# A balanced expert assignment rebuilt: bound instead of range, early choice, four columns a count product, one code per token

## The chip, the cores and the metric

The kernel runs on one core of one Trainium2 chip. The metric is the device time of one execution in microseconds, as the median of several runs. A profile of one further execution gives the span of the instructions and the order of time on each engine: PE (TensorE matrix products; PEld is its weight loading), DVE (VectorE), ACT (ScalarE), POOL (GpSimd), SP (SyncE, which issues transfers), and the DMA queues.

## The reference

Two blocks follow one another. The first is a linear attention with a root-mean-square norm, the second a layer of eight experts whose tokens are assigned greedily and evenly: all pairs of token and expert are taken in falling order of their logit, and a pair counts if the token is free and the expert has fewer than 576 tokens.

```python
q, k, v: (8, 8, 576, 64)    g_norm: (64,)
w_gate: (512, 8)   w1: (8, 512, 1024)   w2: (8, 1024, 512)

kv = einsum('bhsd,bhse->bhde', k, v)
out = einsum('bhsd,bhde->bhse', q, kv)
x = out / sqrt(mean(out*out, -1) + 1e-6) * g_norm     # -> x: (4608, 512)

logits = x @ w_gate                                    # (4608, 8)
order = argsort(-logits.flatten())
for idx in order:
    tok, e = idx // 8, idx % 8
    if assigned[tok] >= 0 or counts[e] >= 576: continue
    assigned[tok] = e; counts[e] += 1

for e in range(8):
    mask = assigned == e
    out[mask] = relu(x[mask] @ w1[e]) @ w2[e]
```

## The kernel before

*Attention.* Batches are loaded in pairs by SP and POOL. `kv_product(b)` makes the products of keys and values and, from the gate weights, the columns that give logits. `token_group(i, j0)` handles three columns of 128 tokens: it transposes q, multiplies, and from the squares (`sq`, `ms`) gets the norm's factor `inv` (L175); POOL scales the rows (`x_sb`, L177) and SP stores them in `x_dram`; DVE scales the logits (`part`, L182) and adds them into `lg` (L186). 12 such groups fill `lg`, 128 partitions by 36 columns by 8 experts (4608 tokens).

*Assignment.* The greedy order is found in eight rounds, and each round closes at least one expert. `choose()` takes for each free token its best open expert (`best`, `mx`). `threshold()` looks for the logit at which the first open expert gets full: in each of 6 steps it lays 44 candidates between two ends, compares all tokens with all of them on DVE (`over`, L316), counts per candidate and expert on PE (36 products of 44 columns, `n_ps`, L323), compares the counts with the room left, sums up how many candidates fill an expert (`k_ps`, L332) and takes the two neighbours as new ends. `assign()` gives the tokens above the upper end their expert, and of those between the ends as many as there is room for (`all_ps`, L363). `fetch(t)` picks the expert that is now closed: its number (`index`, L412) is read by SP, which issues the three transfers of its weights (L417, L419); the rank of each of its tokens is found by products with a triangle (`a_ps`, L423) and with one-hot ranges (`s_ps`, L437), and from these come the row numbers `ids` (L455), with which POOL gathers the rows (`xg`, L460) from `x_dram`. In the last round `rest()` gives out what is left.

*Experts.* `turn(t)` transposes the gathered rows (five blocks, `t_ps`, L485). `layers(t)` runs layer 1 (64 products, `h_ps`, L506), and layer 2 (four blocks of 8 products, `y_ps`, L517, and a half block, L525); ACT and DVE copy the results, and POOL puts the rows (`put`, L490). An f32 product is two records on PE.

*Order.* Attention, `control(0)` and `turn(0)` are ordered by the framework's scheduler. From there PE, DVE and ACT keep the order of the program text, and the assignment for expert t+1 is woven into the products of expert t by hand: each `yield` of `control` gives the PE time (us) that has to be issued before its next part, each product yields its own:

```python
            for used in layers(t):
                ...
                if wait is not None:
                    wait -= used
                    if wait <= 0:
                        wait = next(ctl, None)
```

The turn for expert t+1 stands ahead of the half block of expert t. POOL and SP are ordered by the scheduler throughout. The pools of the assignment and of the experts are placed where attention's pool was, on the right side of SBUF; the weights' pool is on the left.

Of the kernel before, what the change touches and what calls it, by code (L numbers as in the profile page):

```python
# [7 lines left out]
FT = mybir.dt.float32  # L8
# [10 lines left out]
NCAND = 44  # L19
NSTEP = 6  # L20
# [5 lines left out]
def kernel(  # L26
# [31 lines left out]
    wpool = ctx.enter_context(tc.tile_pool(name="wpool", bufs=2, side="left"))  # L58
# [62 lines left out]
    lg = const.tile([P, E, GC], FT, name="lg")  # L121
# [81 lines left out]

    asg = ctx.enter_context(tc.tile_pool(name="asg", bufs=1, side="right"))
# [3 lines left out]
    def bc_e(t):  # L212
        return t.rearrange("p (e o) -> p e o", o=1).to_broadcast([P, E, GC])

    def bc_c(t):
        return t.rearrange("p (o c) -> p o c", o=1).to_broadcast([P, E, GC])

    def small(nm, w=1, dt=FT):
        return asg.tile([P, w], dt, name=nm, tag="s_" + nm, bufs=2)
# [4 lines left out]
    ones_b = asg.tile([P, P], BF, name="ones_b")  # L224
    nc.vector.memset(ones_b, 1.0)
    before = asg.tile([P, P], BF, name="before")
    nc.vector.tensor_scalar(before, in0=row_f, scalar1=iota_p, scalar2=None, op0=AL.is_gt)
    code = asg.tile([P, E], FT, name="code")
    nc.vector.tensor_scalar(code, in0=row_f[:, 0:E], scalar1=-1.0, scalar2=float(E), op0=AL.mult, op1=AL.add)
    inner = asg.tile([P, E, GC], BF, name="inner")  # L230
    nc.vector.memset(inner, 1.0)
    nc.vector.memset(inner[:, :, 0:1], 0.0)
    slot_i = asg.tile([P, NB * P], I32, name="slot_i")
    nc.gpsimd.iota(slot_i, pattern=[[1, NB * P]], base=0, channel_multiplier=0)
    slot_f = asg.tile([P, NB * P], FT, name="slot_f")
    nc.gpsimd.tensor_copy(slot_f, slot_i)
    place_i = asg.tile([P, NB], I32, name="place_i")
    nc.gpsimd.iota(place_i, pattern=[[P, NB]], base=0, channel_multiplier=1)
    place_f = asg.tile([P, NB], FT, name="place_f")
    nc.vector.tensor_copy(place_f, place_i)  # L240


    know = asg.tile([P, 2, GC + 3], BF, name="know")
    for n in range(2):
        nc.vector.tensor_copy(know[:, n, GC + 2:GC + 3], iota_p)


    ends = asg.tile([P, 2], FT, name="ends")
    lgf = lg.rearrange("p e c -> p (e c)")
    nc.vector.tensor_reduce(ends[:, 0:1], lgf, axis=AXX, op=AL.max)  # L250
    nc.vector.tensor_reduce(ends[:, 1:2], lgf, axis=AXX, op=AL.min)
    top = asg.tile([P, 1], FT, name="top")
    bottom = asg.tile([P, 1], FT, name="bottom")
    for n, (t, op) in enumerate(((top, AL.max), (bottom, AL.min))):
        wide = asg.tile([P, P], FT, name="wide", tag="wide", bufs=2)
        nc.vector.tensor_copy(wide, ends[:, n:n + 1].to_broadcast([P, P]))
        end_ps = bank([P, P], "end_ps")
        nc.tensor.transpose(end_ps, wide, ident)
        nc.vector.tensor_reduce(t, end_ps, axis=AXX, op=op)
    above = asg.tile([P, 1], FT, name="above")  # L260
    nc.vector.tensor_tensor(above, top, bottom, op=AL.subtract)
# [32 lines left out]
    code_mx = asg.tile([P, GC], FT, name="code_mx")  # L294

    def choose():


# [280 lines left out]
```

## Time and profile before

| what | us |
|---|---|
| median of 3 runs (lowest, highest) | 846.94 (846.91, 849.73) |
| the profiled execution: its own time | 847.75 |
| its span | 846.0 |
| PE busy, PEld, DVE, ACT, POOL | 714.9, 470.7, 332.4, 152.1, 136.5 |
| attention, to the last logits | 0 to 168 |
| first assignment and gathering | 168 to 237 |
| eight experts | 237 to 836 |

A row of the order of time has the start and the length in us, engine, line, operation, the tiles written and read, shapes, how many instructions are merged in it, and in brackets the idle time of the engine ahead of it with what ended it. A group's row has after the bar its busy us, mean ns of one, and the idle time ahead of it. A row of waits has the us in total, how often, and the longest.

### The profile page before, as it was taken

What the parts mean: (1) busy time and instruction counts of PE and PEld (TensorE: products, weight loads), DVE (VectorE), ACT (ScalarE), POOL (GpSimd) and SP (SyncE); (2) the same over time, 40 slices, a digit from 0 to 9 for tenths busy, and PEclk for the clock granted to TensorE, in tenths of its full rate; (3) what the DMA queues carried; (4) which work ended last, traced back from release to release, by engine and by line L of the source; (5) the groups of instructions that cost most, each with busy time, mean ns of one, the idle gap of its engine ahead of it and who ended that gap; (6) DMA issues with size and microseconds to landing.
All of it is one profiled execution on the core that took longest, in us unless ns stands there. A gap on an engine that the chain in (4) does not pass through costs nothing.

```text
span 846.0 us, 12815 instructions
## 1 busy us (share of the span) xinstructions
PE 714.9 (85%) x5410; PEld 470.7 (56%) x5410; DVE 332.4 (39%) x1033; ACT 152.1 (18%) x310; POOL 136.5 (16%) x119
## 2 busy tenths in 40 slices
PE   0689889513099999999999999999999997999995
PEld 0678778413077447645754674576467545745741
DVE  0064854855725505633570555156235605000000
ACT  0043442400021021102112110211021121202200
POOL 2133523310100210030003003100300031111001
PEclk9899999855599999999999999999999998999998
DMA  9999892100610430070016005300800264200000
GB/s 221 300 243 291 246 295 91 76 38 1 223 32 2 166 139 8 1 284 27 2 57 248 7 2 199 112 2 1 291 20 2 82 223 156 105 25 32 1 25 31
DMA packets 36793, 91.01 MB, mean 108 GB/s; under 512 B 2944, under 2 KB 2944, under 8 KB 36736
## 3 DMA queue, kind: packets, MB, share of 16 engines
q1 hardware_dynamic: 29056, 66.59, 24.0%
q0 software_dynamic: 6976, 23.60, 8.6%
q8 instruction: 42, 0.69, 0.3%
q10 hardware_dynamic: 704, 0.02, 0.1%
q14 instruction: 15, 0.12, 0.0%
HBM read 71.32 MB, written 18.87 MB: 107 GB/s over the span
## 4 chain that ended last, share of the span: by engine, by line
PE 59%; issue 16%; DVE 13%; DMA 6%; ACT 3%; POOL 2%; ACTq 0%; SPq 0%; POOLq 0%; DVEq 0%
PE h_ps L506 24%; PE y_ps L517 17%; PE n_ps L323 6%; DMA v_sb<-in_v_dram 4%; PE o_ps L162 3%; PE y_ps L525 3%; PE kv_ps L131 2%; DVE part L182 2%; DMA w_sb<-in_moe_w_dram 1%; DVE over L316 1%; DVE ms L167 1%; ACT xt L486 1%; PE qt_ps L155 1%; POOL out_dram L490 1%; PE t_ps L485 1%
## 5 line engine op out<-in xcount | busy, mean ns | idle before, releaser
L506 PE MATMUL h_ps<-xt,w_sb 128*128 128x288 f32 x1024 | 273.0, 417 | 0.0
L517 PE MATMUL y_ps<-w_sb,hid 128*128 128x512 f32 x512 | 224.6, 595 | 0.0
L506 PEld LDWEIGHTS h_ps<-xt,w_sb 128*128 128x128 f32 x1024 | 189.4, 191 | 58.2 <-issue 10.6
L517 PEld LDWEIGHTS y_ps<-w_sb,hid 128*128 128x128 f32 x512 | 95.8, 190 | 124.0 <-issue 123.2
L490 POOL DMA_INDIRECT out_dram<-y_sb,ids x40 | 38.7, 966 | 500.0 <-DVE rel L441 293.8
L530 DVE TENSOR_TENSOR y_sb<-y_ps,y_part 64x512 f32<-64x512 f32 x8 | 5.5, 683 | 266.1 <-ACT y_part L529 266.1
L509 ACT ACTIVATE hid<-h_ps 128x288 f32<-128x288 f32 x128 | 52.5, 410 | 260.1 <-PE h_ps L506 258.5
L316 DVE TENSOR_TENSOR over<-mx,cand 128x1584 bf16<-128x1584 f32 x42 | 75.9, 1808 | 1.3
L323 PE MATMUL n_ps<-best,over 128*44 128x8 bf16 x1512 | 50.2, 178 | 19.5 <-DVE over L316 19.5
L323 PEld LDWEIGHTS <-over 128*44 128x44 bf16 x1512 | 46.1, 104 | 36.6 <-DVE over L316 22.7
L131 PE MATMUL kv_ps<-v_sb,k_sb 64*64 64x64 f32 x1152 | 43.0, 235 | 27.5 <-DMA v_sb<-in_v_dram 27.5
L520 ACT COPY y_sb<-y_ps 128x512 f32<-128x512 f32 x32 | 18.7, 585 | 216.3 <-PE y_ps L517 216.3
L131 PEld LDWEIGHTS kv_ps<-v_sb,k_sb 64*64 64x64 f32 x1152 | 40.3, 150 | 30.5 <-issue 25.8
L162 PE MATMUL o_ps<-bd,qt 128*64 128x144 f32 x576 | 46.8, 305 | 11.3 <-DVE qt L157 9.7
L460 POOL DMA_INDIRECT xg<-x_dram,ids x40 | 38.1, 953 | 85.8 <-DVE ids L455 52.0
L162 PEld LDWEIGHTS o_ps<-bd,qt 128*64 128x64 f32 x576 | 38.7, 144 | 15.4 <-ACT o_sb L166 10.5
L177 POOL TENSOR_TENSOR x_sb<-o_sb,inv 128x1536 f32<-128x1536 f32 x12 | 33.2, 2766 | 48.7 <-DVE inv L175 40.1
L326 DVE SCALAR_TENSOR_TENSOR full<-n_ps,goal 44x8 f32<-44x8 f32 x42 | 6.6, 158 | 83.7 <-PE n_ps L323 83.7
L486 ACT ACTIVATE xt<-t_ps,g_col 128x512 f32<-128x512 f32 (+1 forms) x40 | 24.0, 644 | 70.1 <-issue 68.4
L485 PE MATMUL t_ps<-ident,xg 128*128 128x128 f32 (+1 forms) x160 | 23.2, 283 | 14.2 <-DMA xg<-x_dram,ids 9.8
L485 PEld LDWEIGHTS t_ps<-ident,xg 128*128 128x128 f32 (+1 forms) x160 | 18.0, 147 | 23.1 <-DMA xg<-x_dram,ids 9.9
L525 PE MATMUL y_ps<-w_sb,hid 128*64 128x512 f32 x128 | 29.2, 598 | 0.0
(147 smaller groups left out, 466.9 us busy)
## 6 DMA issues: line engine op xcount, KB each, us to landing
w_sb<-in_moe_w_dram SPq DMA_DIRECT2D x16, 1024.0 KB, 6.3
w_sb<-in_moe_w_dram SPq DMA_DIRECT2D x8, 2048.0 KB, 17.3
k_sb<-in_k_dram SPq DMA_DIRECT2D x8, 1152.0 KB, 8.2
v_sb<-in_v_dram SPq DMA_DIRECT2D x8, 1152.0 KB, 12.7
x_dram<-x_sb SPq DMA_DIRECT2D x12, 768.0 KB, 3.8
q_sb<-in_q_dram POOLq DMA_DIRECT2D x4, 1152.0 KB
q_sb<-in_q_dram SPq DMA_DIRECT2D x4, 1152.0 KB
xg<-x_dram,ids POOLq DMA_INDIRECT x40
```

What stands on the lines that cost most here:

```text
L131: nc.tensor.matmul(kv_ps[ls, r, :], lhsT=k_sb[ls, r, j, :], rhs=v_sb[ls, r, j, :], start=(j == 0), stop=(j == R - 1))
L162: nc.tensor.matmul(o_ps[ps_, r, 0:W], lhsT=qt[:, r, ps_], rhs=bd[:, 2 * i + n, r], start=True, stop=True)
L177: nc.gpsimd.tensor_tensor(x_sb.rearrange("p (a l d) -> p a l d", l=2, d=D), o_sb.rearrange("p t r w -> p (t r) w")[:, :, 0:P].rearrange("p ...
L316: nc.vector.tensor_tensor(over, mx.rearrange("p (c o) -> p c o", o=1).to_broadcast([P, GC, NCAND]), cand[:, 1:NCAND + 1].rearrange("p (o n ...
L323: nc.tensor.matmul(n_ps, lhsT=over[:, c, :], rhs=best[:, :, c], start=(c == 0), stop=(c == GC - 1))
L460: nc.gpsimd.indirect_dma_start(out=xg[0:nr, :], out_offset=None, in_=x_dram, in_offset=bass.IndirectOffsetOnAxis(ap=ids[0:nr, n:n + 1], ax ...
L485: nc.tensor.transpose(t_ps[:, d, 0:nr], xg[0:nr, d * P:(d + 1) * P], ident[0:nr, 0:nr])
L490: put = nc.gpsimd.indirect_dma_start(out=out, out_offset=bass.IndirectOffsetOnAxis(ap=ids_of[t][0:nr, n:n + 1], axis=0), in_=y_sb[0:nr, :] ...
L506: nc.tensor.matmul(h_ps, lhsT=w1[:, d, f * P:(f + 1) * P], rhs=xt[:, d, cs], start=(d == 0), stop=(d == DC - 1))
L509: nc.scalar.activation(hid[:, f, cs], h_ps, ACT.Relu)
L517: nc.tensor.matmul(y_ps, lhsT=hid[:, f, a:a + nr], rhs=w2[:, f, :], start=(f == 0), stop=(f == FC - 1))
L525: nc.tensor.matmul(y_ps[l * nr:(l + 1) * nr], lhsT=hid[:, l * FC // 2 + f, a:a + nr], rhs=w2[:, l * FC // 2 + f, :], start=(f == 0), stop= ...
```

## The change

- The logits are no longer searched for their range: from the gate weights comes a bound on any logit (`bound`, with `g2_ps` and a square root), to which the logits are also cut. `top` and `bottom` come from it.
- The pool `asg` moves to the left side and is opened ahead of attention, so that the constants and the first candidates (`cand0`) are made at the start; the weights' pool moves to the right.
- `choose` and the first comparison (`compare` into `over0`) run for columns 0 to 16, 16 to 24, 24 to 32 and 32 to 36 after the token groups that end at columns 18, 24, 33 and 36 (`early`).
- 32 candidates and 7 steps instead of 44 and 6. A count product takes four columns at once: 128 columns of weights (4 columns of tokens by 32 candidates) by 32 streamed (4 by 8 experts); only the four blocks on the diagonal of the result are used, and DVE takes three of them from the room before it compares the fourth.
- `assign` keeps one number per token, `who` (the expert's code), instead of the mask `given`; `index` comes ahead of the tokens' marks; `fetch` compares `who` with the code.
- In `fetch` a difference of ranks (`fall`) replaces the second comparison with 640 slots.
- All yields are set anew; `control(0)` and `turn(0)` are inside the hand-ordered part; expert 0 runs layer 1 by halves of its tokens.

```diff
-NCAND = 44
-NSTEP = 6
+NCAND = 32
+NSTEP = 7
...
-    wpool = ctx.enter_context(tc.tile_pool(name="wpool", bufs=2, side="left"))
+    asg = ctx.enter_context(tc.tile_pool(name="asg", bufs=1, side="left"))
...
+    g2_ps = psa.tile([P, E], FT, name="g2_ps", tag="aux")
+    nc.tensor.matmul(g2_ps, lhsT=ones_f, rhs=g2, start=True, stop=True)
+    bound = asg.tile([P, 1], FT, name="bound")
+    nc.vector.tensor_reduce(bound, g2_ps, axis=AXX, op=AL.max)
+    nc.scalar.activation(bound, bound, ACT.Sqrt)
...
+    def choose(c0=None, c1=GC):
+        cs = slice(c0 or 0, c1)
+        n = cs.stop - cs.start
+        if c0 is None:
+            nc.vector.tensor_tensor(wl, lg, bc_e(shut), op=AL.add)
+        else:
+            nc.vector.tensor_scalar(lg[:, :, cs], in0=lg[:, :, cs], scalar1=bound, scalar2=bottom,
+                                    op0=AL.min, op1=AL.max)
+        w = wl if c0 is None else lg
+        nc.vector.tensor_reduce(mx[:, cs], w[:, :, cs].rearrange("p e c -> p c e"), axis=AXX, op=AL.max)
+        nc.vector.tensor_tensor(pick[:, :, cs], w[:, :, cs], bc_c(mx[:, cs]), op=AL.is_ge)
+        nc.vector.tensor_tensor(pick[:, :, cs], pick[:, :, cs], bc_e(code, n), op=AL.mult)
+        nc.vector.tensor_reduce(code_mx[:, cs], pick[:, :, cs].rearrange("p e c -> p c e"), axis=AXX, op=AL.max)
+        nc.vector.tensor_tensor(best[:, cs].rearrange("p c e -> p e c"), pick[:, :, cs], bc_c(code_mx[:, cs]),
+                                op=AL.is_equal)
+        if c0 is None:
+            nc.vector.tensor_tensor(mx, mx, gone, op=AL.add)
...
         for j0 in range(0, R, T):
             token_group(i, j0)
+            c0 = {18: 0, 24: 16, 33: 24, GC: GC - G}.get(i * R + j0 + T)
+            if c0 is not None:
+                early(c0, (i * R + j0 + T) // G * G)
...
-            yield 6.5 if s == 0 else 2.9
-            n_ps = bank([NCAND, E], "n_ps")
-            for c in range(GC):
-                nc.tensor.matmul(n_ps, lhsT=over[:, c, :], rhs=best[:, :, c], start=(c == 0), stop=(c == GC - 1))
...
-            yield 0.9
+            yield 7.2 if s == 0 else 2.8
+            n_ps = bank([P, G * E], "n_ps")
+            for c in range(0, GC, G):
+                nc.tensor.matmul(n_ps, lhsT=over[:, c:c + G].rearrange("p c n -> p (c n)"),
+                                 rhs=best[:, c:c + G].rearrange("p c e -> p (c e)"),
+                                 start=(c == 0), stop=(c == GC - G))
+            need = goal[0:QP]
+            for g in range(1, G):
+                less = small("need", E)[0:QP]
+                nc.vector.tensor_tensor(less, need, n_ps[g * QP:(g + 1) * QP, g * E:(g + 1) * E], op=AL.subtract)
+                need = less
...
+            yield 1.4
...
-        yield 4.5
+        yield 3.6
+        all_ps = bank([P, 3, E], "all_ps")
...
+        mid = asg.tile([P, E, GC], BF, name="mid", tag="mid")
+        nc.vector.tensor_tensor(mid, two[:, 1], two[:, 0], op=AL.subtract)
...
+        index = small("index", dt=I32)
+        nc.vector.tensor_scalar(index, in0=which, scalar1=-1.0, scalar2=float(E), op0=AL.mult, op1=AL.add)
         nc.vector.tensor_tensor(here, here, bc_e(last), op=AL.is_le)
+        took = small("took", GC)
+        nc.vector.tensor_reduce(took, here.rearrange("p e c -> p c e"), axis=AXX, op=AL.max)
+        nc.vector.tensor_tensor(took, took, cut[:, 0], op=AL.max)
+        mine = small("mine", GC)
+        nc.vector.tensor_tensor(mine, took, code_mx, op=AL.mult)
+        nc.vector.tensor_tensor(who, who, mine, op=AL.max)
...
-        yield 3.0
+        own = small("own", GC)
+        nc.vector.tensor_scalar(own, in0=who, scalar1=which, scalar2=None, op0=AL.is_equal)
+        along = small("along", GC, BF)
+        nc.vector.tensor_tensor_scan(along, ones_b[:, 0:GC], own, 0.0, op0=AL.mult, op1=AL.add)
+        yield 5.5 if t < E - 1 else 8.0
+        a_ps = bank([P, GC + 1], "a_ps")
+        nc.tensor.matmul(a_ps[:, 0:1], lhsT=before, rhs=along[:, GC - 1:GC], start=True, stop=True)
+        nc.tensor.matmul(a_ps[:, 1:GC + 1], lhsT=fall, rhs=along, start=True, stop=True)
...
-        yield 2.4
+        yield 1.5
...
-        for f in range(FC):
-            for c in range(2):
+        for f, c in [(f, c) for f in range(FC) for c in range(2)] if t else [(f, c) for c in range(2) for f in range(FC)]:
+            if True:
...
-    for _ in control(0):
-        pass
-    for _ in turn(0):
-        pass
     with tc.manual_schedule(engines={mybir.EngineType.PE, mybir.EngineType.DVE, mybir.EngineType.Activation}):
+        for _ in control(0):
+            pass
+        for _ in turn(0):
+            pass
```

More of the change, by code (lines that the diff above doesn't have):

```diff
@@ L235 @@
[L235 to L259, printed above, removed]
@@ new lines, in threshold @@
+            nc.tensor.matmul(k_ps, lhsT=ones_b[0:QP, :], rhs=some, start=True, stop=True)
+            ends = small("ends", 2)
+            hi, lo = ends[:, 0:1], ends[:, 1:2]
+            for n in range(2):
+                at = small("at", NCAND + 1)
+                nc.vector.scalar_tensor_tensor(at, in0=row_f[:, 0:NCAND + 1], scalar=k_ps, in1=cand[:, n:NCAND + 1 + n],
+                                               op0=AL.is_equal, op1=AL.mult, accum_out=ends[:, 1 - n:2 - n])
+        return ends
@@ L375, in assign @@
-        nc.vector.tensor_scalar(is_full, in0=room, scalar1=0.5, scalar2=None, op0=AL.is_lt)
+        nc.vector.scalar_tensor_tensor(last, in0=left, scalar=-1.0e6, in1=all_ps[:, 2], op0=AL.add, op1=AL.subtract)
+        fresh = small("fresh", E)
+        nc.vector.scalar_tensor_tensor(fresh, in0=over_room, scalar=0.5, in1=code_left, op0=AL.is_lt, op1=AL.mult)
+        which = small("which")
+        nc.vector.tensor_reduce(which, fresh, axis=AXX, op=AL.max)
+        index = small("index", dt=I32)
```

297 lines of the change are left out of this document (146 added, 151 removed).

## The prediction

> **What bounds the kernel now.** I read the page's slices first, then the busy time by stages, then the order of time of each engine, then the waits. The columns of a stage are its length, then PE, PEld, DVE, ACT and POOL busy (instructions), granted clock, DMA share, GB/s.
>
> ```profile
> DVE  0064854855725505633570555156235605000000
> 174.40:184.20 9.80, 0.66 (x2) 0.29 (x2) 9.30 (x42) 0.00 (x0) 1.24 (x3) 0.50 0.00 0
> 184.20:210.80 26.60, 10.57 (x222) 9.76 (x223) 14.73 (x57) 0.00 (x0) 0.00 (x0) 0.50 0.00 1
> 210.80:237.30 26.50, 4.75 (x29) 3.70 (x28) 15.80 (x56) 2.55 (x4) 4.86 (x5) 0.52 0.56 203
> 314.40:700.00 385.60, 374.15 (x2292) 227.36 (x2290) 168.92 (x570) 61.84 (x130) 47.94 (x50) 1.00 0.24 86
> ```
>
> Attention ends near 168 us. From there to 237 us PE waits for the first assignment, at a granted clock of 0.50: 69 us bound by a chain of small DVE and PE work. From 314.4 to 700 us five experts take 385.60 us, 77.12 us each, and PE is busy for 97% of it: there the time is what stands in PE's queue. So the change counts in two ways: the length of the exposed chain, and the PE time and PE stalls that each later assignment puts among the experts' products.
>
> ```profile
> 161.39 2.76 POOL L177 TENSOR_TENSOR x_sb<-o_sb,inv 128x1536 f32<-128x1536 f32 x1 [3.79 <-DVE inv L175]
> 162.09 2.27 DVE L182 TENSOR_TENSOR part<-o_sb,inv 128x192 f32<-128x192 f32 x1
> 167.28 0.36 DVE L182 TENSOR_TENSOR part<-o_sb,inv 128x192 f32<-128x192 f32 x1
> 167.67 0.50 DVE L186 TENSOR_REDUCE lg<-part 128x24 f32<-128x192 f32 x1
> 167.85 2.76 POOL L177 TENSOR_TENSOR x_sb<-o_sb,inv 128x1536 f32<-128x1536 f32 x1 [3.71 <-DVE part L182]
> 174.43 0.17 DVE L225 MEMSET ones_b<- 128x128 bf16 x1 [6.26 <-DMA x_dram<-x_sb]
> 184.22 1.60 PE L323 MATMUL n_ps<-best,over 128*44 128x8 bf16 x36 [6.61 <-DVE over L316]
> 188.99 1.60 PE L323 MATMUL n_ps<-best,over 128*44 128x8 bf16 x36 [2.57 <-DVE over L316]
> 210.82 0.24 DVE L347 TENSOR_SCALAR cut<-mx,hi 128x36 f32<-128x36 f32 x1
> 217.38 0.15 DVE L412 TENSOR_SCALAR index<-which 128x1 int32<-128x1 f32 x1
> 227.16 0.17 DVE L455 SCALAR_TENSOR_TENSOR ids<-got,col 128x5 int32<-128x5 f32 x1
> 232.96 3.67 PE L485 MATMUL t_ps<-ident,xg 128*128 128x128 f32 x16 [9.77 <-DMA xg<-x_dram,ids]
> 237.26 7.06 PE L506 MATMUL h_ps<-xt,w_sb 128*128 128x288 f32 x28
> ```
>
> The last logits are written at 168.17, but the first instruction of the assignment (`ones_b`) starts at 174.43: it waits for the last store of x to DRAM, because its pool takes the place of attention's. The first count starts at 184.22, a step takes 4.77 us (184.22 to 188.99), the thresholds are done at 210.8, the expert's index at 217.51, the row numbers at 227.33, the first product of layer 1 at 237.3.
>
> ```profile
> 246.57 3.18 PE L506 MATMUL h_ps<-xt,w_sb 128*128 128x288 f32 x12
> 249.68 1.13 PE L323 MATMUL n_ps<-best,over 128*44 128x8 bf16 x36
> 250.74 1.24 PE L506 MATMUL h_ps<-xt,w_sb 128*128 128x288 f32 x4
> 252.01 0.75 PE L506 MATMUL h_ps<-xt,w_sb 128*128 128x288 f32 x2
> 284.05 0.16 PE L423 MATMUL a_ps<-know,before 128*128 128x1 bf16 x1 [1.70 <-DVE index L412]
> 286.73 0.29 PE L437 MATMUL s_ps<-know,of 128*128 128x39 bf16 x5
> 286.87 20.85 PE L517 MATMUL y_ps<-w_sb,hid 128*128 128x512 f32 x48
> 708.32 0.16 PE L423 MATMUL a_ps<-know,before 128*128 128x1 bf16 x1 [4.64 <-DVE index L412]
> 708.34 5.15 PE L506 MATMUL h_ps<-xt,w_sb 128*128 128x288 f32 x10
> 766.52 1.04 PE L485 MATMUL t_ps<-ident,xg 128*128 128x128 f32 x8
> 773.35 31.31 PE L506 MATMUL h_ps<-xt,w_sb 128*128 128x288 f32 x128
> 832.06 3.65 PE L525 MATMUL y_ps<-w_sb,hid 128*64 128x512 f32 x16
> PE a_ps L423 <- DVE index L412: 10.2, 6, 1.7
> ```
>
> This is PE among the experts. One step of a threshold goes from 246.57 to 252.01, 5.44 us, with 16 records (8 products) of layer 1 in it. Expert 7 has no assignment beside it: 128 records take 31.2 us, 0.2435 each, so 8 products are 3.90 us and a step costs 1.54 us of PE: 1.06 for the 36 count products (249.68 to 250.74), 0.48 for `k_ps` and the gaps at the changes between f32 and bf16. Besides, `a_ps` waits 1.7 us for DVE six times (10.2 us), and 4.64 us at 708.32 for the last assignment.
>
> **The change, part by part.**
>
> *Start of the chain.* The pool moves away from attention's, constants are built while attention's first loads run (DVE's first two slices, 42 us, are empty), and the bound comes from the gate weights instead of the logits; the end transposes and most of the 42 DVE instructions of that stage, the choice over all 36 columns among them (174.43 to 182.3), go. What stays behind the last logits is the choice and comparison of four columns: six operations of 32 elements and one of 128. The price of small ones:
>
> ```profile
> L368 DVE TENSOR_TENSOR last<-left,all_ps 128x8 f32<-128x8 f32 x7 | 1.1, 162 | 0.2
> L182 DVE TENSOR_TENSOR part<-o_sb,inv 128x192 f32<-128x192 f32 x12 | 19.6, 1634 | 0.1
> L316 DVE TENSOR_TENSOR over<-mx,cand 128x1584 bf16<-128x1584 f32 x42 | 75.9, 1808 | 1.3
> L406 DVE TENSOR_TENSOR own_e<-given,hot 128x288 bf16<-128x288 bf16 x8 | 3.7, 457 | 0.2
> ```
>
> A dependent small one takes 0.16 and starts 0.04 to 0.1 later, so 0.24 each. But the four two-input ones meet POOL's `x_sb`: `part` takes 0.36 at 167.28, before POOL starts, and 2.27 at 162.09, where it ends with POOL's operation (164.15); the group's mean is 1634 ns. So I take the clip and the first maximum at once, a block until POOL's end at 170.61, then five at 0.27 and 0.04 to PE: 172.0. To this comes what the earlier three parts (16, 8 and 8 columns) cost attention itself: about 2.2, 1.5 and 1.5 us of DVE plus a POOL operation (2.76) in front of each at worst, with the last part 15 us as an upper bound; below, nothing (DVE is given work only). DMA is still the limit for the first part, and DVE has gaps, so nearer to the lower end: 2.5. First count at 174.5 instead of 184.22: -9.7.
>
> *Steps.* Seven instead of six. The comparison falls from 1584 elements (1.81) to 1152; 1.65 x 1152/1584 and 0.16 fixed, 1.36. Nine count products replace 36. At 232 us and before, the clock is half:
>
> ```profile
> 222.84 0.35 PE L437 MATMUL s_ps<-know,of 128*128 128x39 bf16 x5 [2.69 <-DVE know L433]
> 227.61 1.08 POOL L460 DMA_INDIRECT xg<-x_dram,ids  x1 [51.97 <-DVE ids L455]
> 232.78 0.91 POOL L460 DMA_INDIRECT xg<-x_dram,ids  x1 [0.30 <-issue]
> ```
>
> Five `s_ps` products with 128 columns of weights and 39 streamed take 0.35; one alone (`a_ps`) takes 0.16, so they come some 47 ns apart and nine are 0.53, against 1.60. Three subtractions come between count and comparison, 0.20 each. A step: 0.56 count, 0.60, 0.20, 0.20, 0.20 to `k_ps`' readers, 0.38 for both ends, 0.28 for candidates, 1.42 for the comparison: 3.84. Six of them and a last one without candidates and comparison (2.3) are 25.3 against 26.6 (184.22 to 210.8): -1.3, and -2.5 to +1 if a subtraction is 0.15 or 0.3.
>
> *Split.* From the ends to the index: 0.28 for both cuts, 0.87 for two products, 0.79 and 0.1 for the sums, then, ahead of the room in DVE's order, the difference, the scan and the scaled sum (1.63), and 1.05 for six small ones: 4.7 against 6.7: -2.0. From the index to the row numbers no other work is mixed in any more, and one comparison of 36 codes replaces product and reduction over 288: 6.2 against 9.8. The rows come no sooner than DMA allows: the weights' 4 MB start with the index and the gathers meet them. Before, the last gather was issued at 232.78 and layer 1 began at 237.3. Bounds: 0 (rows held until the weights are in) and -3.6 (all of it); gathers have a queue of their own, so I take -3.0. In expert 0 the order of layer 1 by halves changes nothing, since all turning products stand ahead of it.
>
> *Among the experts.* Per step PE does nine products. Warm, five `s_ps` go from 286.73 to 286.87, 28 ns each: 0.26 for nine against 1.06. With `k_ps` and the gaps a step is 0.74, seven 5.2, against 9.3. The rest: `all_ps`, `a_ps`, `s_ps` 0.5 with no stall. Base without assignment: 773.35 to 835.65 is 62.3, and the turn and its gaps 766.52 to 769.77, 3.25: 65.5. So 71.2 instead of 77.12: -5.9, six times -35.5. Between a count and the one before, `k_ps` to count is paced by six products (2.92) for 0.47 + 0.28 + 1.36 = 2.1 of DVE; count to `k_ps` by three (1.46) for 1.0; `a_ps` by seven of layer 2 (6.0, at 0.434 a record) for 3.4; the first count by 15 (7.3) for some 6.6: 1.35 until `y_sb` is added, seven operations of the choice with 288 elements at 0.45 to 0.65, then candidates and comparison. These covers hold the edits that cost nothing; without them each costs its whole DVE time.
>
> *Last assignment.* 8.0 of pacing is 17 products (8.28) for 6.5 of DVE: the stall of 4.64 goes, and what followed it: ten records took 5.15 instead of 2.44 at a clock that had fallen. 65.5 + 0.5 against 73.3 (700.0 to 773.35): -7.3.
>
> *What moves.* The index comes after ten products of layer 2 instead of one, and the row numbers after 19 instead of 8: 13 products, 11.2 us, remain to the turn. SP then issues three weight transfers, POOL five gathers of 1.25 us each behind two of the output puts.
>
> ```profile
> w_sb<-in_moe_w_dram SPq DMA_DIRECT2D x8, 2048.0 KB, 17.3
> ```
>
> The weights land 17.3 after issue and layer 1 of the next expert starts some 19 after the index's issue, but needs `w2` 31 us later still: covered. The last gather is issued 2.9 + 5.0 us after `s_ps` and may take 4.5 (232.78 to 237.3 holds its landing, turning and copy): 12.4, needed at 11.2 + 2.85 = 14.0. Covered by 1.6 us only.
>
> Sum: 9.7 + 1.3 + 2.0 + 3.0 + 35.5 + 7.3 = 58.8. The profiled execution took 847.75 (span 846.0): 789.0, and the median 846.94 is 0.8 below it: 788.
>
> **A rule against it.** A count product loads 128 columns of weights where it loaded 44. By the rows the load hides: 28 ns for 128 columns (`s_ps`) and 29 for 44. The Trainium skill, TensorE: Matmul & The Clock Gate, LDWEIGHTS, has the load's time grow with its columns, P/1.2 ns, 107 ns for 128. By that nine are 0.96 and the sum would be about 30 us smaller. The trace's `s_ps` row does not bear it out.
>
> **The rivals.**
> - *Weights by column.* If a count product were paid by its weight columns, 1.06/36 x 128/44 = 86 ns, nine are 0.77, +0.51 on 42 warm steps and +0.55 on seven cold ones: +25.6, 814. For it: 44-column loads at half clock need 41 ns each. Against: both `s_ps` rows. 6%.
> - *Gathers late.* If the gathers, 8 us later in layer 2, share DMA worse than I take, PE waits at the turn: 2 us at each of six, 12 in all: 800. For it: DMA was busy for 0.56 of 26.5 us in expert 0's start, 14.8 us, and the gathers now come in the middle of such a stretch. 13%.
> - *Attention pays.* All four parts at their upper bound, 15 instead of 2.5: 801. For it: the 1634 ns of `part`. Against: DVE's gaps there. 8%.
> - *Slower.* POOL's queue is in order and not written by hand. If the put of layer 2's fourth block stands ahead of the gathers, they start after 32 products: 0.65 + 1.3 + 5.0 to the last issue and 4.5 to its use, where 2.85 was due, so PE waits some 9 us at each of six turns, with clocks lost as at 708 (2.7 each): +70, 858. It decides from 9.8 us lost per turn. Against: gathers are ready at the 22nd product, that put at the 33rd. 3%.
> - *No effect.* The stalls only move, from `a_ps` to the next wait: 10.2 + 4.64 and the 2.7 of clock stay, 17.5: 806. For it: the split's chain is barely shorter. Against: seven products of cover instead of four. 4%.
>
> **How the numbers follow.** My forecast 64%, with 781 to 796 by its own bounds: attention 0 to 8, gathers -3.6 to 0, gaps 0.28 to 0.39 a step. The range takes in late gathers and attention's price: 780 to 806. No measurement of this kernel tells less than 0.5% (4 us) from no change. Faster: all but the slower rival and 2% for what I do not see, 0.95; same 0.02, slower 0.03.
>
> **What would show it.** The first count near 174.5 and 3.8 us a step; layer 1 of expert 0 near 221; 71.2 us from expert to expert; `n_ps` groups of nine in some 0.4 with their tail; no wait of `a_ps` for DVE; no wait of `t_ps` for gathers beyond the first. Wrong it is if `n_ps` groups take 0.9, if PE's waits name `over`, `some` or the gathers, or if attention ends after 172.

## The result, and the profile after

The runs of each kernel are compared with runs of the kernel before on the same chip.

| kernel | median us (lowest, highest) | ratio to before, 95% interval |
|---|---|---|
| before, beside after | 848.34 (846.91, 850.56) | |
| after | 790.33 (789.52, 792.82) | 0.9319 (0.9286 to 0.9352) |

The forecast was 788.0, within 780 to 806. After's profiled execution took 792.82 (span 791.0) against before's 847.75 (846.0): 54.9 us less between the two profiles. The page's slices and the same stages as before, of after (columns: length, PE, PEld, DVE, ACT, POOL busy, granted clock, DMA share, GB/s):

```profile
DVE  0364746587825625562663455165445514000000
177.70:182.40 4.70, 0.20 (x2) 0.20 (x2) 4.07 (x13) 0.00 (x0) 2.06 (x1) 0.50 0.41 166
182.40:205.10 22.70, 3.63 (x61) 2.49 (x60) 17.27 (x82) 0.00 (x0) 0.00 (x0) 0.50 0.01 1
205.10:229.60 24.50, 5.58 (x31) 3.89 (x31) 15.55 (x51) 2.59 (x4) 6.23 (x5) 0.50 0.60 219
301.30:652.60 351.30, 348.42 (x1542) 206.87 (x1540) 171.91 (x690) 61.82 (x130) 48.78 (x50) 1.00 0.27 94
```

DVE's second slice (about 20 to 40 us), empty before, has work in it now; the first is still empty. Five experts take 351.30 us where they took 385.60, 70.26 each, with 750 PE records fewer; PE is busy for 99% of it. The order of time of after's exposed chain (PE and DVE):

```profile
177.18 0.50 DVE L319 TENSOR_REDUCE lg<-part 128x24 f32<-128x192 f32 x1
177.72 2.08 DVE L225 TENSOR_SCALAR lg<-lg,bound,bottom 128x32 f32<-128x32 f32 x1
181.20 0.18 PE L364 MATMUL n_ps<-best,over 128*128 128x32 bf16 x1 [4.42 <-DVE best L232]
184.64 0.42 PE L364 MATMUL n_ps<-best,over 128*128 128x32 bf16 x9 [2.09 <-DVE cand L358]
188.32 0.42 PE L364 MATMUL n_ps<-best,over 128*128 128x32 bf16 x9 [2.09 <-DVE cand L358]
205.15 0.23 DVE L392 TENSOR_TENSOR cut<-mx,ends 128x72 bf16<-128x72 f32 x1
209.78 0.15 DVE L425 TENSOR_SCALAR index<-which 128x1 int32<-128x1 f32 x1
229.58 9.04 PE L552 MATMUL h_ps<-xt,w_sb 128*128 128x288 f32 x30
```

Against the rows of before that the prediction shows, the thresholds are done at 205.15 instead of 210.82, the index comes at 209.78 instead of 217.38, layer 1 of expert 0 starts at 229.58 instead of 237.26. But the last logits are written at 177.68 instead of 168.17. Attention itself became 9.5 us longer, and where the rows come from is seen here (after, DVE, POOL and PE):

```profile
102.22 0.50 DVE L319 TENSOR_REDUCE lg<-part 128x24 f32<-128x192 f32 x1
102.03 2.78 POOL L310 TENSOR_TENSOR x_sb<-o_sb,inv 128x1536 f32<-128x1536 f32 x1 [2.98 <-DVE inv L308]
102.76 2.13 DVE L225 TENSOR_SCALAR lg<-lg,bound,bottom 128x128 f32<-128x128 f32 x1
106.34 0.41 DVE L266 COPY bd<-kv_ps 64x256 f32<-64x256 f32 x1
107.20 1.12 PE L270 MATMUL t_ps<-ident,bd 128*128 128x128 f32 x4 [5.05 <-ACT bd L267]
111.33 6.20 PE L264 MATMUL kv_ps<-v_sb,k_sb 64*64 64x64 f32 x124
```

The same place in before:

```profile
102.64 0.40 DVE L133 COPY bd<-kv_ps 64x256 f32<-64x256 f32 x1
103.50 0.66 PE L137 MATMUL t_ps<-ident,bd 128*128 128x128 f32 x4 [1.34 <-ACT bd L134]
105.83 3.83 PE L131 MATMUL kv_ps<-v_sb,k_sb 64*64 64x64 f32 x124
```

Up to 102.7 the two kernels run alike. Then the first early part stands in DVE's queue ahead of the copy `bd`. Its first operation, the clip of the logits to the bound, takes 2.13 us: it ends with POOL's `x_sb` (104.81). `bd` comes 3.70 us later, PE waits 5.05 instead of 1.34 us, and after that wait the same 124 records of `kv_ps` take 6.20 instead of 3.83 us, at a granted clock of 0.50 from 107.2 to 116 us where before has 1.00 (over the stretch from 100 to 120 us the mean is 0.74 against 1.00). So 3.6 us of DVE time ahead of `bd` cost 7.9 us: `kv_ps` ends at 117.53 instead of 109.66.

Among the experts (after, PE):

```profile
281.27 0.17 PE L475 MATMUL a_ps<-along,before 128*128 128x1 bf16 x1
294.49 1.04 PE L530 MATMUL t_ps<-ident,xg 128*128 128x128 f32 x8
313.69 0.38 PE L364 MATMUL n_ps<-best,over 128*128 128x32 bf16 x9
313.92 1.70 PE L552 MATMUL h_ps<-xt,w_sb 128*128 128x288 f32 x6
315.65 3.18 PE L552 MATMUL h_ps<-xt,w_sb 128*128 128x288 f32 x12
318.67 0.38 PE L364 MATMUL n_ps<-best,over 128*128 128x32 bf16 x9
652.60 8.51 PE L552 MATMUL h_ps<-xt,w_sb 128*128 128x288 f32 x34
660.95 0.17 PE L475 MATMUL a_ps<-along,before 128*128 128x1 bf16 x1
718.40 6.82 PE L552 MATMUL h_ps<-xt,w_sb 128*128 128x288 f32 x27
```

A step is 4.98 us (313.69 to 318.67) with 18 records of layer 1 in it; at 0.2435 a record these are 4.38, so the step costs PE 0.60. Nine count products hold it for 0.23 (313.69 to 313.92), 26 ns each. Neither `a_ps` row has idle time, and the turn at 294.49 has none ahead of it: both the old stall and the late gathers are absent. In the waits of PE over the whole execution, `a_ps` (4.3 us) and `t_ps` (0.6 us for the gathers) each wait once, both ahead of expert 0.

### The profile page after: what moved, and what is told of

It is laid out like the page before. It is cut to its first block, busy times and chain, and to the rows that moved or that the text cites. A ratio compares the mean times of both kernels' runs of the same rounds, so it can differ in the third digit from the quotient of the medians.

```text
span 791.0 us, 10903 instructions
## 1 busy us (share of the span) xinstructions
PE 681.3 (86%) x4361; PEld 443.4 (56%) x4361; DVE 344.7 (44%) x1214; ACT 151.1 (19%) x310; POOL 138.3 (17%) x118
## 4 chain that ended last, share of the span: by engine, by line
PE 59%; issue 19%; DVE 11%; DMA 5%; ACT 2%; POOL 2%; POOLq 0%; ACTq 0%; DVEq 0%
PE h_ps L552 27%; PE y_ps L563 16%; PE o_ps L295 4%; DMA v_sb<-in_v_dram 4%; PE kv_ps L264 3%; PE y_ps L571 3%; DVE part L315 2%; PE n_ps L364 1%; DVE ms L300 1%; PE qt_ps L288 1%; DVE over L238 1%; PE w_ps L275 1%; POOL out_dram L535 1%; PE t_ps L530 1%; ACT xt L531 1%
## 5 line engine op out<-in xcount | busy, mean ns | idle before, releaser
L563 PE MATMUL y_ps<-w_sb,hid 128*128 128x512 f32 x512 | 227.2, 597 | 0.0
L535 POOL DMA_INDIRECT out_dram<-y_sb,ids x40 | 39.7, 993 | 441.3 <-ACT y_sb L566 390.7
L238 DVE TENSOR_TENSOR over<-mx,cand 128x1152 bf16<-128x1152 f32 (+3 forms) x52 | 67.0, 1289 | 1.6
L264 PE MATMUL kv_ps<-v_sb,k_sb 64*64 64x64 f32 x1152 | 45.2, 242 | 0.1
L264 PEld LDWEIGHTS kv_ps<-v_sb,k_sb 64*64 64x64 f32 x1152 | 42.4, 156 | 3.2 <-issue 2.9
L364 PEld LDWEIGHTS <-over 128*128 128x128 bf16 x441 | 18.1, 97 | 38.4 <-DVE over L238 22.4
L370 DVE TENSOR_TENSOR need<-goal,n_ps 32x8 f32<-32x8 f32 x49 | 7.5, 154 | 69.0 <-PE n_ps L364 69.0
L364 PE MATMUL n_ps<-best,over 128*128 128x32 bf16 x441 | 19.2, 178 | 21.4 <-DVE cand L358 12.5
L385 DVE SCALAR_TENSOR_TENSOR at<-row_f,k_ps,cand 128x33 f32<-128x33 f32 x98 | 21.5, 257 | 34.3 <-PE k_ps L380 34.3
```

Of the source, the lines that this page charges most:

```text
L238: nc.vector.tensor_tensor(over[:, c0:c1], mx[:, c0:c1].rearrange("p (c o) -> p c o", o=1).to_broadcast([P, c1 - c0, NCAND]), cand[:, 1:NCA ...
L264: nc.tensor.matmul(kv_ps[ls, r, :], lhsT=k_sb[ls, r, j, :], rhs=v_sb[ls, r, j, :], start=(j == 0), stop=(j == R - 1))
L364: nc.tensor.matmul(n_ps, lhsT=over[:, c:c + G].rearrange("p c n -> p (c n)"), rhs=best[:, c:c + G].rearrange("p c e -> p (c e)"), start=(c ...
L535: put = nc.gpsimd.indirect_dma_start(out=out, out_offset=bass.IndirectOffsetOnAxis(ap=ids_of[t][0:nr, n:n + 1], axis=0), in_=y_sb[0:nr, :] ...
L563: nc.tensor.matmul(y_ps, lhsT=hid[:, f, a:a + nr], rhs=w2[:, f, :], start=(f == 0), stop=(f == FC - 1))
```

## The experiments

**The first early part.** `e1_gap` makes it wait for batch 4's logit columns, `e2_noearly` has no early part at all.

```diff
+        if i == 2:
+            late = asg.tile([P, 1], FT, name="late")
+            nc.vector.scalar_tensor_tensor(late, in0=bd[:, 4, 0, P:P + 1], scalar=0.0, in1=bound, ...)
+            early(0, 16, late)
-            c0 = {18: 0, 24: 16, 33: 24, GC: GC - G}.get(i * R + j0 + T)
+            c0 = {24: 16, 33: 24, GC: GC - G}.get(i * R + j0 + T)      # e1_gap
+            c0 = {GC: 0}.get(i * R + j0 + T)                           # e2_noearly; it has no `if i == 2` part
...
```

> The first early part (columns 0 to 16) is made to wait for the logit columns of batch 4, so that DVE does it in its gap beside PE's next products of keys and values, when POOL is idle. Theory A (the clip to the bound is held by POOL's x_sb for 2.1 us, the copy that PE waits for comes 3.7 us late behind it, PE idles 5 us and then runs at half clock, 4.2 us more): PE's products of the fifth batch take 3.8 us again instead of 6.1, the last logits come near 170 us instead of 177.7, and the time falls by 7.5 from 790.3 to 783. Theory B (DVE's added work costs attention the same wherever it stands): 789 to 790, last logits still near 177.

> No early parts: choice and first comparison for all 36 columns after the last logits, everything else as in the changed kernel. Theory A: last logits near 168.5, then the clip waits for POOL until 171, choice and comparison take 5.5, first k_ps near 177 instead of 182.4: 785, so the early parts are a loss of 5 us. Theory C (attention is later because of the constants and the bound at its start, not because of the early parts): last logits near 177, first k_ps near 186: 794.

`e1_gap`: 783.09 us (782.83 to 784.74), ratio 0.9256 (0.9231 to 0.9281). `e2_noearly`: 784.86 (782.51 to 786.11), 0.9264 (0.9234 to 0.9293). In the order of time of `e1_gap`:

```profile
105.79 0.35 DVE L225 TENSOR_SCALAR lg<-lg,late,bottom 128x128 f32<-128x128 f32 x1
105.23 3.83 PE L264 MATMUL kv_ps<-v_sb,k_sb 64*64 64x64 f32 x124
168.56 0.50 DVE L319 TENSOR_REDUCE lg<-part 128x24 f32<-128x192 f32 x1
```

The clip of the same 128 columns takes 0.35 without POOL beside it, `kv_ps` runs in 3.83 again, and the last logits come at 169.06, 0.9 us after before's. In `e2_noearly` they come at 167.11, but the choice over 36 columns then stands in the chain:

```profile
174.35 0.42 PE L364 MATMUL n_ps<-best,over 128*128 128x32 bf16 x9 [12.87 <-DVE best L232]
```

So the early parts, as placed, lose more than they bring: without them the kernel is 5.5 us faster by the medians (the intervals, 0.9234 to 0.9293 and 0.9286 to 0.9352, just touch), and layer 1 of expert 0 starts at 222.82 instead of 229.58. That moving the first part alone brings the gain is clear of the scatter (`e1_gap` ends at 0.9281). What the parts are worth when well placed is not: 1.8 us by the medians (784.86 to 783.09, inside the runs' scatter), 2.1 by the start of layer 1 (222.82 and 220.68).

**What halves the speed of `kv_ps`.** `e7_warm` puts products that nothing reads (20 of them) into PE's queue behind the sixth token group.

```diff
+            if i * R + j0 + T == 18:
...
+                for _ in range(20):
+                    nc.tensor.matmul(warm, lhsT=ident, rhs=inv, start=True, stop=True)
```

> Twenty products whose result nobody reads stand in PE's queue where it waits for the first early part (they need the norm's factor, ready at 101.8). DVE's order is unchanged, so the copy that PE waits for still comes near 106.4. Theory A (of the 7.9 us, 4.2 are PE's clock, which falls in the idle time): PE's products of the fifth batch take 3.8 us instead of 6.1, last logits near 174, time 786. Theory E (the products are slow because DVE or DMA feed them late): they still take 6 us, 790.

790.5 us, one execution. The order of time on PE and DVE:

```profile
98.82 7.61 PE L337 MATMUL warm<-inv,ident 128*128 128x24 f32 x40 [2.00 <-DVE inv L308]
106.36 2.61 PE L264 MATMUL kv_ps<-v_sb,k_sb 64*64 64x64 f32 x42
109.01 0.42 DVE L266 COPY bd<-kv_ps 64x256 f32<-64x256 f32 x1 [5.21 <-PE kv_ps L264]
112.77 3.83 PE L264 MATMUL kv_ps<-v_sb,k_sb 64*64 64x64 f32 x124
```

The edit does more than keep PE at work. The filling products stand ahead of the last 42 `kv_ps` records that `bd` needs, so `bd` comes 9.27 us after the clip's start, where it was 3.58 in after, and the time is no evidence. The granted clock fell here too: it is 0.50 from 100 to 110 us, while PE is busy with the filling products, behind 2.00 us of idle time. It is back at 1.00 when the 124 records start, and they take 3.83 although `bd` was later than in after. So the clock, and not a late feed by DVE or DMA (whose share is near 1.0 beside the 124 records in both), makes them slow in after.

That the idle time lets the clock fall is not shown by this run, only by comparing the others. In the seven profiles with the first part ahead of `bd` and no filling (after, `e3_last`, `e4_hold`, `e6_single`, `e8_flat`, `e10_act`, `e13_w2`), PE waits 3.51 to 5.06 us for `bd`, and the 124 records take 5.10 to 6.54. In the six with `bd` first (before, `e5_pace`, `e1_gap`, `e2_noearly`, `e11_best`, `e12_both`) it waits 1.34 or 1.35, and they take 3.83. In between the length alone does not decide: in before, the granted clock is 0.53 behind 2.14 us of idle time at 126.88, and 1.00 behind 2.06 at 94.56.

**POOL's hold on the last part.** `e3_last` issues the last `x_sb` behind the last early part; `e10_act` lets ACT scale those rows.

```diff
+            if i * R + j0 + T == GC:
+                rows()        # e3_last: x_sb and its store for the last group, held back by best
...
+        if i * R + j0 + T == GC:      # e10_act
+            for k in range(T * H):
+                nc.scalar.mul(x_sb[:, k * D:(k + 1) * D], o_sb[:, t, r, l * D:(l + 1) * D], inv[:, k:k + 1])
```

> POOL scales the last three columns of rows only after the last early part is done (its factor is copied behind that part). Theory A: the last clip takes 0.2 instead of 2.08, first k_ps at 180.5 instead of 182.4, the rows are in DRAM 4 us later, 30 us before the first gather: 1.8 us less, 788.5. Theory D (the end of the chain to layer 1 is set by transfers, not by the assignment): layer 1 starts at 229.6 as now, 790.

> After, with one operation moved: the rows x of the last token group are scaled by ACT (24 pieces of 64 columns) instead of POOL, so that no POOL operation runs while DVE does the last clip, choice and comparison. Theory A (POOL's operation holds DVE's clip, 2.08 us against 0.30 without POOL): the last clip takes 0.3, the first two threshold steps come 3.68 apart as the others, and from the end of the last logits to all_ps it takes 28.2 us instead of 30.0; the time falls by 1.8, to about 788.5. Rival B (the 2.08 us are the clip's own, or come from the store of the rows): the clip stays at 2.1 and the stretch at 30.0. Rival C (ACT's pieces make the rows late for the gathers): layer 1 of expert 0 comes later after the index than 19.8 us.

`e3_last`: 790.31 us in one execution. The clip took 0.30 there, but POOL then held a later operation of the first step, `at`, which finds one of the two new ends (1.81 us, the next one 0.25), and the count behind that came late:

```profile
177.57 2.76 POOL L324 TENSOR_TENSOR x_sb<-o_sb,inv_late 128x1536 f32<-128x1536 f32 x1 [6.66 <-DVE need L382]
178.56 1.81 DVE L397 SCALAR_TENSOR_TENSOR at<-row_f,k_ps,cand 128x33 f32<-128x33 f32 x1 [0.25 <-PE k_ps L392]
182.17 0.42 PE L376 MATMUL n_ps<-best,over 128*128 128x32 bf16 x9 [3.65 <-DVE cand L370]
```

3.65 instead of 2.09 us: the block moved, and from the last logits to `all_ps` it took 29.76 instead of after's 30.01. `e10_act` (788.32, one execution) takes POOL out:

```profile
174.95 5.83 ACT L313 ACTIVATE x_sb<-o_sb,inv 128x64 f32<-128x64 f32 x24 [1.66 <-DVE inv L308]
175.83 0.30 DVE L225 TENSOR_SCALAR lg<-lg,bound,bottom 128x32 f32<-128x32 f32 x1
```

From the last logits (175.79) to `all_ps` (204.01) it is 28.22, where 28.2 was expected: POOL's operation, not the clip, was the 1.8 us.

**From the index to layer 1 of expert 0.** In after, POOL and PE, and what DMA moved from 205 to 240 us (40 slices of 0.875 us, GB/s):

```profile
216.98 1.14 POOL L506 DMA_INDIRECT xg<-x_dram,ids  x1 [37.22 <-DVE shut L440]
221.60 1.62 POOL L506 DMA_INDIRECT xg<-x_dram,ids  x1 [0.30 <-issue]
226.73 2.92 PE L530 MATMUL t_ps<-ident,xg 128*128 128x128 f32 x12 [0.57 <-DMA xg<-x_dram,ids]
GB/s 0 0 0 0 0 0 0 0 70 183 403 410 405 393 389 391 374 360 405 396 379 363 426 386 377 33 0 0 0 0 0 0 0 0 0 0 0 19 0 0
DMA packets 2465, 5.39 MB, mean 154 GB/s; under 512 B 128, under 2 KB 128, under 8 KB 2464
```

Two suspects: issues of which four take 1.14 to 1.62 us with DVE at work beside them (in before all five took 1.08 to 0.91), or DMA, which moves 5.39 MB at some 400 GB/s without a gap until the last rows are there. `e4_hold` keeps DVE still until the last gather has landed; `e13_w2` asks for the second-layer weights (2.1 MB) only then.

```diff
+        if t == 1:      # e4_hold, ahead of choose(): DVE waits for the last gather of expert 0
+            nc.vector.tensor_copy(held, last_rows[0][0:1, 0:1])
+            nc.vector.scalar_tensor_tensor(shut[0:1, 0:1], in0=held, scalar=0.0, in1=shut[0:1, 0:1], ...)
...
+        if t == 0:      # e13_w2, behind the gathers; w2's own request now stands under t > 0
+            nc.gpsimd.tensor_copy(w2[0:1, 0, 0:1], xg[0:1, 0:1])
+            nc.sync.dma_start(w2, moe_w2[bass.ds(e, 1)]...)
```

> After, with one thing added: DVE's choice for expert 1 starts only when the last gather of expert 0 has landed. Theory A (the gathers of expert 0 are issued slowly, 1.14 to 1.62 us each, because DVE's work runs beside POOL's, where before they took 0.91 to 1.08): the five issues fall back to about 5.0 us in all from 6.4, layer 1 of expert 0 starts 1 us earlier, and the time falls by about 1, to 789 (seen in the stretch from the thresholds to layer 1: 18.8 instead of 19.8 us). Rival B (the issue is slow for the transfers that run at the same time, or the turn waits for something else): the issues stay at 1.1 to 1.6 us, and the stretch stays at 19.8 within 0.3.

> After, with one transfer moved: the second-layer weights of expert 0 (2 of its 4 MB) are requested only when the last gather of its rows has landed. In after, 5.4 MB (4.2 of weights, 1.2 of rows) move between the index and layer 1 of expert 0, and layer 1 starts 19.8 us after the index, though the row numbers are ready 3.6 us sooner than in before. Theory A (the volume holds the rows: with 5.4 MB at 0.4 MB per us the last rows come at the end of the stretch whenever they are asked for): with 2.1 MB less ahead of them layer 1 starts 17 to 18.5 us after the index, and the time falls by about 2, to 788. Rival B (POOL's slow issues, the last one ending 14.65 us after the index, set it together with landing and turning): 19.5 within 0.4, time as in after.

`e4_hold`, 789.39 us in one execution: the issues fall to 1.08 to 0.91, yet layer 1 starts 19.36 us after the index (206.69) instead of 19.80, and 19.5 to 19.7 in the other kernels with after's order:

```profile
215.28 0.98 POOL L507 DMA_INDIRECT xg<-x_dram,ids  x1 [0.31 <-issue]
226.05 6.26 PE L558 MATMUL h_ps<-xt,w_sb 128*128 128x288 f32 x18
```

`e13_w2`, 789.05 in one execution, index at 207.75:

```profile
225.39 9.46 PE L556 MATMUL h_ps<-xt,w_sb 128*128 128x288 f32 x30
GB/s 0 0 0 0 0 0 77 293 407 412 410 386 375 126 211 94 206 187 112 122 220 108 0 7 169 131 311 393 410 365 410 201 0 19 0 0 0 0 0 0
```

17.64 us, within what the volume theory gave, and the DMA falls to 94 to 220 GB/s while only rows are under way: now the issues are what is left, as `e12_both` shows below. `e4_hold`'s half of the theory (faster issues) held, its gain did not come.

**Among the experts: spacing and packing.** `e5_pace` is the kernel before, with its six steps, and one `yield` altered (5.2, and 8.0 at the last expert, for 3.0); `e6_single` is after with single-column counts.

```diff
-        yield 3.0
+        yield 5.2 if t < E - 1 else 8.0          # e5_pace, in before's fetch
...
+            n_ps = bank([QP, E], "n_ps")             # e6_single; no subtractions
+            for c in range(GC):
+                nc.tensor.matmul(n_ps, lhsT=over[:, c], rhs=best[:, c], start=(c == 0), stop=(c == GC - 1))
```

> The kernel before, with one number altered: while the seven steps of an expert's choice wait, the fetch of that expert gives up 5.2 (8.0 at the last expert) of the work under way between steps instead of 3.0, so that the seven steps reach as far into the expert under way as DVE's late work on the logits did not allow. Theory A (part of what the change brought among the experts could have been had by spacing alone): the turn's wait of the products behind DVE, which costs some 2 to 3 us an expert in before, shrinks, and the time falls by about 17 us, to 830. Rival B (the wait only moves: DVE's own work for an assignment, not the spacing, is what PE waits for): within 3 us of before, 844 to 850. Rival C (the later thresholds make the gathers late and the turn waits for them): slower, 850 to 860.

> After, with the count made by 36 products of one column each in place of nine products of four columns, and without the three subtractions that take the diagonal blocks together; everything else as in after, the spacing of the steps too. It tells what the packing of columns is worth by itself. Theory A (each product costs its fixed 22 to 25 ns and the step keeps PE for all of them): a warm step takes 36 x 0.025 = 0.9 instead of 0.23 us of PE, and with 42 warm steps among the experts the time rises by 42 x 0.67 = 28 us; the seven cold steps ahead of expert 0 lose 7 x 1.2 and win back 7 x 0.6 for the subtractions, about 4; in all 790 + 32 = 822 (815 to 830). Rival B (the cost of a step among the experts is the wait around the count, not its products, because DVE's part is shorter without the subtractions): 790 to 798.

`e5_pace`: 828.76 us (827.55 to 831.47), ratio 0.9797 (0.9775 to 0.9820) to a before of 846.4. `a_ps` waits no longer:

```profile
697.00 0.17 PE L423 MATMUL a_ps<-know,before 128*128 128x1 bf16 x1
```

and an expert takes 75.27 us instead of 77.12. So 17.6 us were to be had in the old kernel by altering one `yield`. `e6_single`: 827.94 (827.56 to 828.04), 0.9781 (0.9764 to 0.9797), 37.6 more than after:

```profile
313.37 1.06 PE L364 MATMUL n_ps<-best,over 128*32 128x8 bf16 x36
314.35 1.72 PE L546 MATMUL h_ps<-xt,w_sb 128*128 128x288 f32 x6
319.22 1.06 PE L364 MATMUL n_ps<-best,over 128*32 128x8 bf16 x36
```

The step is 5.85 us with the same 18 records, 1.47 of its own instead of 0.60: 42 x 0.87 = 36.5, and the cold steps 3.80 instead of 3.68, 0.8 in seven. These 37.3 us are nearly the whole of the measured difference of 37.6: taking the packing of four columns out of after costs more than half of what the change brings. Without it seven steps cost 10.3 us an expert, more than before's six at 1.54 (9.2).

**The strided marks.** `e8_flat` writes `best` in the order in which it lies in memory.

```diff
-        nc.vector.tensor_tensor(best[:, cs].rearrange("p c e -> p e c"), pick[:, :, cs], ...)
+        nc.vector.tensor_tensor(best[:, cs], pick[:, :, cs].rearrange("p e c -> p c e"), ...)
```

> After, with the comparison that makes the bf16 marks of the best expert written in the order in which it lies in memory (columns, then experts), its inputs read with a stride instead. Theory A (the 1448 ns that the 288-element comparison takes come from the strided bf16 output): the row falls to 0.45 to 0.70 us, and the time stays within 2 us of 790, since among the experts DVE's choice lies beside PE's layers. Rival B (the strided side costs the same whether it is read or written): the row stays above 1.2 us.

791.69 us in one execution. The groups of DVE's work by shape, of after:

```profile
L232 DVE TENSOR_TENSOR best<-pick,code_mx 128x288 bf16<-128x288 f32 x7 | 10.1, 1448 | 0.2
```

and of `e8_flat`:

```profile
L232 DVE TENSOR_TENSOR best<-pick,code_mx 128x288 bf16<-128x288 f32 x7 | 4.6, 662 | 0.2
```

0.79 us less in each of seven operations and nothing in the time: among the experts the choice lies beside PE's work.

**Together.** `e11_best` has the edits of `e1_gap`, `e10_act` and `e4_hold`, `e12_both` that of `e13_w2` as well.

> After, with three edits: the first early part waits for the products of batch 4 (as in e1_gap), the rows of the last token group are scaled by ACT (as in e10_act), and DVE's choice for expert 1 waits for the last gather of expert 0 (as in e4_hold). Theory A (the three lie in different stretches of one chain and add up): 783.1 - 1.8 - 0.4 = 781 (779 to 783), 0.923 of before, and 9 us under after. Rival B (the gaps that the first edit closes already hold the other two): 783 to 785.

> The three edits of e11_best (19.6 us from the index to layer 1 of expert 0) with the moved transfer of e13_w2. Theory A (volume): layer 1 16.5 to 17.5 us after the index, since the issues end 1.3 us sooner than in e13_w2 and are now what is left; the time falls from 781.2 by 2.2 to about 779 (777 to 780.5). Rival B (volume does not matter): 19.6 and 781. Rival C (the second-layer weights come too late for layer 2 of expert 0, or push the weights of expert 1 back): over 782, with a wait of y_ps for the transfer.

`e11_best`: 781.15 us (779.73 to 782.49), 0.9227 (0.9207 to 0.9247). `e12_both`: 778.07 (776.99 to 781.95), 0.9203 (0.9183 to 0.9223), the fastest version run. In it (index at 197.18):

```profile
213.89 8.92 PE L571 MATMUL h_ps<-xt,w_sb 128*128 128x288 f32 x30
```

16.71 us after the index, against 17.64 in `e13_w2`: with the volume out of the way, the faster issues are now worth 0.9 us. The step from 781.15 to 778.07 is near the scatter of the runs (the intervals overlap by 0.0016); that it comes from this stretch is seen in the rows, 19.60 against 16.71.

What the bound, the moved pool, the codes in `who` and `fall` bring was not run one by one.

## Why the prediction was right

The direction and the main step, what a count costs PE among the experts, were right for the reason given. That the total came within 4 us is in part luck: the start of the chain and the gathers brought 8.2 us less than forecast, the experts 4.2 us more. Between the profiled executions:

| step | predicted | measured | rows |
|---|---|---|---|
| start of the chain and steps | -11.0 | -5.7 | thresholds 210.82 to 205.15 |
| split | -2.0 | -1.9 | thresholds to index 6.56 to 4.63 |
| row numbers and gathers | -3.0 | -0.1 | index to layer 1 19.88 to 19.80 |
| among the experts | -35.5 | -39.7 | 237.26 to 700.02, now 229.58 to 652.60 |
| last assignment | -7.3 | -7.5 | 73.33 to 65.80 |
| sum | -58.8 | -54.9 | |

*What failed: attention's price.* The rival "attention pays" was more than half true: 9.5 us where the sum had 2.5 and the bound was 15. The sum took DVE's gaps as cover and looked at the cost on DVE alone. The rows show that a part put ahead of `bd` is paid by PE, once as waiting (3.7 us) and once more as half clock (4.2), 7.9 us for the first part alone; `e1_gap` brings these back by moving it. In other executions the loads come up to 3 us sooner, so the price is best counted from the logits of the sixth group (written from 102.22 on in both profiles): to the end of the last logits it is 65.95 us in before, and 74.35 to 75.76 in the seven profiles with after's first part where it was and no filling. That is a price of 8.4 to 9.8, in no case 2.5. In `e1_gap` the same stretch is 67.43, a price of 1.5: the sum's 2.5 would have been enough for parts that are well placed. The prediction's own sign of being wrong here, attention ending after 172, came (177.68), and its marks for the chain, a first count near 174.5 and layer 1 of expert 0 near 221, were missed: the count that ends the early parts starts at 181.20, layer 1 at 229.58. The Trainium skill, TensorE: Matmul & The Clock Gate, What's actually happening, has the clock halved after an idle window of about 3.4 us. At this place the rows agree, with 5.05 us idle ahead of the slow `kv_ps` and 1.34 ahead of the full-speed one; that it also fell behind 2.00 us (`e7_warm`) and 2.14 (before) is less than such a window. The prediction, which had seen a fallen clock at 708 us, did not ask for it in attention.

*What failed in it: whom POOL holds.* The prediction laid POOL's hold on "the four two-input ones" and let the clip pass at once. The clip, with one tensor input, was held for 2.13 and 2.08 us against 0.35 and 0.30. The sum of the last part came out all the same (3.5 us from the last logits to the last count product, 3.8 by the prediction), since the block is only met one operation earlier. The Trainium skill, SBUF — State Buffer, Who interferes with whom, names `tensor_scalar` among the operations that can take the port pair shared with GpSimd; `e10_act` agrees.

*What failed: the gathers.* Both bounds were named, 0 ("rows held until the weights are in") and -3.6, and -3.0 was taken because "gathers have a queue of their own". The measured -0.1 is the other bound, and `e13_w2` shows why: a queue of its own does not bring the rows ahead of 4.2 MB of weights. The last full block of rows is there (226.73) when the whole transfer ends (the slices fall at 226.9), and with 2.1 MB less ahead of it layer 1 comes 2.2 us sooner. The Trainium skill, DMA: Bandwidth & Descriptors, Queues, rings and completion order, has each DMA engine take turns between the queues packet by packet; no run here shows the order of the packets.

*What was too careful.* An expert takes 70.26 us, not 71.2: nine products were 0.23 (predicted 0.26), and two changes between f32 and bf16 with `k_ps` some 0.37 instead of 0.48. The cold step was 3.68 instead of 3.84.

*What held.* A count product is not paid by its 128 weight columns (26 ns each): the rival of 814 is refuted, and so are the 107 ns a product that the prediction set against its own sum. The wait of `a_ps` and the 4.64 at the last assignment went as priced (17.5 in the "no effect" rival, 17.6 in `e5_pace`). The gathers were in time at each turn, so neither "gathers late" nor the slower case came.

## What to carry to other kernels

Where work is put into the gaps of an engine that is "only half busy", look at what stands behind it in that engine's queue: here a copy of 0.4 us that PE waits for made 3.6 us of DVE time cost 7.9. Before a transfer is taken for hidden because it has its own queue, add up all bytes under way in that stretch; asking later for those that are needed later brought expert 0's first product 2 to 3 us forward. And try the spacing of interleaved work before rebuilding it: one `yield` in the old kernel gave 17.6 us, while the whole change gave 58. The count of four columns in one small product is worth more: without it after is 37.6 us slower.

## What was not expected of the hardware

- A DVE operation with one tensor input (the clip) was held by POOL's two-input operation, 2.13 us against 0.35 at 128 columns, and 2.08 against 0.30 at 32.
- A 288-element comparison took 1448 ns with a bf16 output strided by 16 bytes, 662 with the inputs strided instead, and 455 with neither (before's `best`, same size). The Trainium skill, SBUF — State Buffer, Door 1: The DMA port swizzle, gives SBUF lines of 16 bytes and a penalty for each access that goes to a new one; each write here does, and that the read side costs far less is not in it.
- Four of POOL's five indirect gathers took 1.14 to 1.62 us to issue with DVE's choice beside them and 0.95 to 1.08 without (`e4_hold`); the fifth, of 64 rows, took 0.91 in both.
- The granted clock fell to half behind idle stretches of PE of about 2 us in some places (2.00 in `e7_warm`, 2.14 at 126.88 in before) and not in others (2.06 at 94.56 in before).
- Nine warm products with 128 bf16 weight columns and 32 moving ones came 26 ns apart (0.23 us); 36 with 32 and 8 came 27 ns apart (0.98 us, `e6_single`): in these two shapes a product has one price.
